# Strassen's seven block products in the second product of an attention and MLP kernel (batches 2 to 7 and the state tokens)

## The chip, the cores and the metric

The kernel runs on one core of a Trainium2 chip. The metric is the device time of one execution in microseconds (us). An engine's name is short for: PE = TensorE, DVE = VectorE, ACT = ScalarE, SP = SyncE, which only issues DMAs here.

## The reference

There are 8 batches of 512 tokens, 8 heads of 64 columns, and 32 state tokens for each batch and head. Tokens attend to the state, and the state attends to the tokens; all 4,608 rows of 512 columns that come out go through an MLP.

```python
scores = x @ state.T / sqrt(D);   a  = softmax(scores);   xread = a @ state
scores2 = state @ x.T / sqrt(D);  a2 = softmax(scores2);  sread = a2 @ x
t = concatenate([xread, sread])            # 8 x (512 + 32) rows of 8 x 64 = 512 columns
h = t @ w_in                               # 512 -> 2048
g = h * tanh(log1p(exp(h)))                # mish
out = g @ w_out                            # 2048 -> 512
```

## The kernel before

**Precision.** Operands of the large products are float32, split into a high part and a low part that TensorE takes (`fp32r`). A product of two such operands is three matmuls: high by high, high by low, low by high. So `gh` and `gl` are the high and low half of the activation `g`, `wo[j][:, :, 1]` and `wo[j][:, :, 0]` those of `w_out`, `swh` and `swl` those of the product named next.

**First product.** `xread @ w_in` is worked out as `a` times (state times `w_in`). `sw_slice` makes the inner product for a slot (32-row matmuls into `swp`, then a cast on ACT to `swh` and a subtraction on DVE to `swl`), and `gemm1` multiplies it by the attention weights, `ah` and `al`, into two banks `ph` of 512 tokens. A slot `j` is 256 of the 2048 hidden columns: two feature chunks of 128. Eight slots make a batch.

**Activation and second product.** ACT takes mish of the two banks into `g` (128x1024, one buffer), DVE casts `g` to `gh` and subtracts to get `gl`, and `gemm2` adds the slot's part of `g @ w_out` to four banks `acc`, one for each tile of 128 tokens: 4 tiles x 2 chunks x 3 matmuls of 512 columns. After slot 7 the banks are copied to `o` and stored. Second products run `LAG` = 2 slots behind the first ones, half of a slot's `acc` in front of a pause, half behind it, and in the pause stand (`beside`) the small groups of the next batch: `swp`, the scores `sc`, the state read `srp`. The state tokens of all batches are gathered (`srds`, turned by `sreads_transposed` into `srT`) and go through `gemm1_s` and four slots of their own between batches 6 and 7.

**Order.** For batch 0 the string `STEPS` is an order by hand of all pieces, DVE and ACT included: `p` a first product, `m` mish and cast of `g`, `lg` its `gl`, `g` a second product, `ji`/`jo`/`lo` joining, casting and splitting a slice of `w_in` or `w_out`, `hi`/`ci`/`di`/`ho`/`co`/`do` roundings of the loaded words. From batch 1 on (`dve.on = act.on = False`) the order on DVE and ACT comes from the scheduler; PE keeps the order of the code. `w_in` joined lies whole in SBUF (`w_in_sb`). All loads and stores go through SP's queue in order.

Of the kernel before, what the change touches and what calls it, by code (L numbers as in the profile page):

```python
# [17 lines left out]
P = 128  # L18
# [67 lines left out]
def state_attention_mish_kernel(ctx, tc, x_turned, x, state_wide, state, w_in, w_out, out):  # L86
# [34 lines left out]
    w_in_sb = const.tile([P, NC, DF], F32, name="w_in_sb")  # L121
# [4 lines left out]
    srT = [const.tile([P, NC, B * NS], F32R, name=f"srT_{n}") for n in ("h", "l")]  # L126
# [56 lines left out]
    def join_w_in(e, raw):  # L183
        join_words(raw, w_in_sb[:, :, e * 2 * P:(e + 1) * 2 * P])
# [142 lines left out]
    def attention(b):  # L327
        aT = {}

        def scores(bank=misc):  # L330
# [8 lines left out]
            soft["sc"] = pool.tile([P, 2, S], F32, tag="sc", name=f"scs_{b}", bufs=2)  # L339
# [54 lines left out]
        def soft1_a():  # L394
# [3 lines left out]
            hi, lo = (pool.tile([P, 2, S], F32R, tag=t, name=f"{t}_{b}") for t in ("ah", "al"))  # L398
# [5 lines left out]
        def softs():  # L404
# [4 lines left out]
            whole(soft1_n(), soft1_a())  # L409
# [17 lines left out]
        def alone(step):  # L427
# [3 lines left out]
            sc=lambda _: scores(second_bank if b == 0 else misc), tr=alone(soft1_t), em=alone(soft2_m), ex=alone(soft1_x),  # L431
            ee=alone(soft2_x), no=alone(soft1_n), pr=alone(soft1_a), tl=alone(soft2_t), sr=sread, aT=aT, softs=softs)
# [3 lines left out]
    def sreads_transposed():  # L436
        for bs in (range(0, 4), range(4, B)):
# [10 lines left out]
    def sw_slice(b, j, n=2, bank=misc):  # L448

        pw = [bank(f"swp_{b}_{j}_{u}")[:, :n * 2 * P] for u in two]  # L450
        for i in range(n):
            f, to = (slice(q * 2 * P, (q + 1) * 2 * P) for q in (j + i, i))
            for c in range(NC):
                o = slice(c * NS, (c + 1) * NS)
                for u in two:
                    last["PE"] = pe.matmul(
                        pw[u][o, to], bd(b, u, c), w_in_sb[half(u), c, f], start=True, stop=True)
        yield
        hi = pool.tile([P, 2, n * 2 * P], F32R, tag="swh", name=f"swh_{b}_{j}", bufs=3)
        lo = pool.tile([P, 2, n * 2 * P], F32R, tag="swl", name=f"swl_{b}_{j}", bufs=3)  # L460
# [314 lines left out]
```

## Time and profile before

| | before |
|---|---|
| median of the runs shown (lowest, highest) | 651.73 us (651.31, 651.95) |
| the profiled execution: its own time / span | 650.5 us / 648.7 us |
| PE busy | 639.4 us, 99% |
| PE weight loads busy (beside matmuls) | 510.1 us, 79% |
| DVE busy | 320.7 us, 49% |
| ACT busy | 234.6 us, 36% |
| granted TensorE clock over the span | 1.000 |

Busy times are those of the profiled execution, over its whole span. A PE that is busy 99% is not thereby at its peak, since matmuls are pipelined and their ends are modelled; how long a stream of them takes is read from where one piece of the chain starts and the next one does. Shares of DVE and ACT are means over stages that differ: they are high in the first 95 us and low later.

### The profile page before, as it was taken

What the parts mean: (1) busy time and instruction counts of PE and PEld (TensorE: products, weight loads), DVE (VectorE), ACT (ScalarE), POOL (GpSimd) and SP (SyncE); (2) the same over time, 40 slices, a digit from 0 to 9 for tenths busy, and PEclk for the clock granted to TensorE, in tenths of its full rate; (3) what the DMA queues carried; (4) which work ended last, traced back from release to release, by engine and by line L of the source; (5) the groups of instructions that cost most, each with busy time, mean ns of one, the idle gap of its engine ahead of it and who ended that gap; (6) DMA issues with size and microseconds to landing.
All of it is one profiled execution on the core that took longest, in us unless ns stands there. A gap on an engine that the chain in (4) does not pass through costs nothing.

```text
span 648.7 us, 10258 instructions
## 1 busy us (share of the span) xinstructions
PE 639.4 (99%) x4380; PEld 510.1 (79%) x4380; DVE 320.7 (49%) x412; ACT 234.6 (36%) x364; POOL 0.7 (0%) x6
## 2 busy tenths in 40 slices
PE   7999999999999999999999999999999999999997
PEld 5776777787778887787778788787778789878886
DVE  5989984293428234543437234742447244332222
ACT  4997862352325122522324213412334234131110
POOL 0000000000000000000000000000000000000000
PEclk9999999999999999999999999999999999999999
DMA  8968115021031003110220003110110001000001
GB/s 329 392 211 337 66 33 204 25 72 28 33 105 68 24 1 130 66 33 1 76 107 27 21 15 116 66 33 1 66 66 23 11 1 66 1 17 17 0 1 65
DMA packets 18573, 47.91 MB, mean 74 GB/s; under 512 B 3424, under 2 KB 7904, under 8 KB 16608
## 3 DMA queue, kind: packets, MB, share of 16 engines
q1 hardware_dynamic: 18384, 47.13, 20.5%
q8 instruction: 34, 0.56, 0.3%
q10 hardware_dynamic: 144, 0.13, 0.1%
q14 instruction: 11, 0.09, 0.0%
HBM read 34.14 MB, written 8.91 MB: 66 GB/s over the span
## 4 chain that ended last, share of the span: by engine, by line
PE 88%; DVE 2%; ACT 2%; issue 1%; DVEq 0%; ACTq 0%
PE acc L78 50%; PE ph L78 24%; PE swp L78 4%; PE acc_s L78 3%; PE ph_s L78 3%; PE srp L78 1%; PE sc L78 1%; ACT L78 1%; DVE w L78 0%; DVE gl L78 0%; ACT g L78 0%; DVE wo L78 0%; ACT wir L78 0%; ACT scs L78 0%; ACT wor L78 0%
## 5 line engine op out<-in xcount | busy, mean ns | idle before, releaser
L78 PE MATMUL acc<-wo,gh 128*128 128x512 f32 (+1 forms) x1028 | 319.5, 392 | 0.0
L78 PEld LDWEIGHTS acc<-wo,gh 128*128 128x128 f32 x1028 | 190.5, 188 | 47.1 <-issue 8.2
L78 PE MATMUL acc<-wo,gl 128*128 128x512 f32 (+1 forms) x514 | 199.9, 389 | 0.1
L78 ACT ACTIVATE g<-ph 128x512 f32<-128x512 f32 x128 | 74.0, 597 | 230.2 <-DVE gl L78 215.9
L78 DVE CAST gh<-g 128x1024 fp32r<-128x1024 f32 x64 | 44.0, 687 | 145.5 <-PE acc L78 141.1
L78 PEld LDWEIGHTS acc<-wo,gl 128*128 128x128 f32 x514 | 96.5, 188 | 21.4 <-DVE gl L78 0.9
L78 DVE TENSOR_TENSOR gl<-g,gh 128x1024 fp32r<-128x1024 f32 x64 | 78.0, 1219 | 4.6
L78 PE MATMUL ph<-ah,swh 128*128 128x512 f32 (+1 forms) x260 | 79.4, 388 | 0.0
L78 PE MATMUL ph<-al,swh 128*128 128x512 f32 (+1 forms) x260 | 78.9, 386 | 0.4 <-DVE al L78 0.4
L78 PE MATMUL ph<-ah,swl 128*128 128x512 f32 (+1 forms) x260 | 78.9, 387 | 0.0
L78 DVE TENSOR_TENSOR swl<-swp,swh 128x512 fp32r<-128x512 f32 (+1 forms) x72 | 41.1, 625 | 64.3 <-ACT swh L78 64.2
L78 PEld LDWEIGHTS ph<-al,swh 128*128 128x128 f32 x260 | 48.4, 188 | 10.5 <-DVE al L78 0.6
L78 PEld LDWEIGHTS ph<-ah,swh 128*128 128x128 f32 x260 | 48.2, 188 | 10.6 <-issue 0.8
L78 PEld LDWEIGHTS ph<-ah,swl 128*128 128x128 f32 x260 | 48.4, 188 | 10.1 <-DVE swl L78 0.2
L78 ACT CAST swh<-swp 128x512 fp32r<-128x512 f32 (+1 forms) x72 | 34.2, 550 | 38.7 <-PE swp L78 38.7
L78 ACT ACT_TABLE_LOAD x27 | 34.6, 1283 | 18.2 <-DVE nm L78 14.7
L78 PE MATMUL swp<-w_in_sb,bds 64*32 64x256 f32 x896 | 28.1, 380 | 0.0
L78 DVE STREAM_TRANSPOSE e<-scs 128x1024 f32<-128x1024 f32 x7 | 8.7, 1244 | 34.6 <-ACT scs L78 34.6
L78 PE MATMUL ph_s<-srT_h,w 128*128 128x256 f32 x128 | 23.9, 286 | 0.4 <-DVE w L78 0.3
L78 ACT COPY o<-acc 128x512 f32<-128x512 f32 (+1 forms) x16 | 9.2, 574 | 40.6 <-PE acc L78 38.7
L78 PEld LDWEIGHTS swp<-w_in_sb,bds 64*32 64x32 f32 x896 | 15.9, 106 | 10.0 <-issue 6.0
L78 DVE COPY o<-acc 128x512 f32<-128x512 f32 (+1 forms) x17 | 11.4, 671 | 21.5 <-PE acc L78 16.1
(64 smaller groups left out, 399.8 us busy)
## 6 DMA issues: line engine op xcount, KB each, us to landing
wir<-in_w_in_dram SPq DMA_DIRECT2D x16, 512.0 KB, 9.1
wor<-in_w_out_dram SPq DMA_DIRECT2D x16, 512.0 KB, 9.3
x<-in_x_dram SPq DMA_DIRECT2D x8, 1024.0 KB, 5.0
out_dram<-o SPq DMA_DIRECT2D x31, 256.0 KB, 2.0
xT<-in_x_turned_dram SPq DMA_DIRECT2D x7, 1024.0 KB, 4.9
e2T<-e2b SPq DMA_DIRECT2D x128, 32.0 KB, 1.9
xT<-in_x_turned_dram SPq DMA_DIRECT2D x2, 512.0 KB, 5.1
out_dram<-o_s SPq DMA_DIRECT2D x2, 256.0 KB, 2.0
```

The costliest lines, as they stand in the source:

```text
L78: made = method(*args, **kwargs)
```

## The change

In batches 2 to 7 and for the state tokens the second product is done in steps (batch, slot, pair `p` of token tiles). In a step the activation is a 2 by 2 block matrix (two tiles of 128 tokens, two chunks of 128 hidden columns) and so is the slice of `w_out` (two chunks, two halves of 256 columns). Strassen's scheme in Winograd's form needs seven products of blocks in place of eight, each again three matmuls, and sums of blocks on both sides:

- `combine_g` forms four sums of 128x128 on DVE, casts the seven left blocks to `gh` on ACT (384 and 512 columns) and subtracts to `gl` on DVE (384 and 512 columns). Mish is now put into unit tiles `gu` by 256 columns.
- `combine_w_out` forms the right blocks once per slot: two adds of 512 columns that bring back `w_out` from its halves, four of 256, four casts on ACT and four subtractions of 256 on DVE.
- `products` are 21 matmuls of 256 columns in place of 12 of 512, and `results` adds the seven sums up at the end of a batch's token pair (five adds of 256 and one of 512 columns on DVE, two copies on ACT).

To make room, `w_in` is no longer kept whole: its eight slices are written to DRAM (`keep_w_in`) and come back two at a time through one buffer (`load_kept`, 1 MB each, four for each of batches 2 to 7 and four for the state tokens). `srT`, `xT` from batch 3 on and `x` share one buffer; `ah`, `al` have one instead of two; `swh`, `swl` two instead of three. First products of a batch stand at steps −2 to 5 of the batch's 16 (slot 0 of batches 3 to 6 at step −8, at the change of token pair of the batch before), `swp` and `sc` at steps of their own. In `STEPS` and `LOADS` pieces change places: three casts of `gh` and two of `wo` go from DVE to ACT (`n`, `ko`), two roundings from ACT to DVE.

```diff
-    w_in_sb = const.tile([P, NC, DF], F32, name="w_in_sb")
+    wi = {}
+    w_in_kept = [dram.tile([P, 2, NC, 2 * P], F32, name=f"w_in_kept_{i}") for i in range(SLOTS // 2)]
...
+    def load_kept():
+        if order:
+            b, i = order.pop(0)
+            w = pool.tile([P, 2, NC, 2 * P], F32, tag="wis", name=f"w_in_{b}_{i}", bufs=1)
+            nc.sync.dma_start(w.rearrange("p j c f -> p (j c f)"), w_in_kept[i].rearrange("p j c f -> p (j c f)"))
+            kept.append(w)
...
+    def combine_w_out(j):
+        w = [new_unit(f"w_{j}_{k}").rearrange("p a n -> p (a n)") for k in two]
+        for k in two:
+            dve.tensor_add(w[k], as_f32(wo[j][:, k, 0]), as_f32(wo[j][:, k, 1]))
+        (b11, b12), (b21, b22) = ((w[k][:, :256], w[k][:, 256:]) for k in two)
...
+        dve.tensor_sub(t1, b12, b11)
+        dve.tensor_sub(t3, b22, b12)
+        dve.tensor_sub(t2, b22, t1)
+        dve.tensor_sub(t4, b21, t2)
+        to = [wo[j][:, 0, :, 256:], wt23[:, 0], wt23[:, 1], wt4[j // 4][:, j % 4]]
+        for part, o in zip((t1, t2, t3, t4), to):
+            act.copy(o[:, 1], part)
+            dve.tensor_sub(o[:, 0], part, as_f32(o[:, 1]))
...
+    def combine_g(step):
+        u = units.pop(step)
...
+        dve.tensor_add(s[:, 0], a21, a22)
+        dve.tensor_sub(s[:, 2], a11, a21)
+        dve.tensor_sub(s[:, 1], s[:, 0], a11)
+        dve.tensor_sub(s[:, 3], a12, s[:, 1])
...
+        for to, of in ((slice(0, 3), u[:, 1:4]), (slice(3, 7), s)):
+            act.copy(gh[:, to], of)
+        for to, of in ((slice(0, 3), u[:, 1:4]), (slice(3, 7), s)):
+            dve.tensor_sub(gl[:, to], of, as_f32(gh[:, to]))
...
+    def products(step, which):
...
+        for name, i in PRODUCTS[which]:
+            bank, side = PLACES[name]
+            o = accs[key, p][bank][:, side * 256:(side + 1) * 256]
+            for n, (g, w) in enumerate(((gh, 1), (gh, 0), (gl, 1))):
+                last["PE"] = pe.matmul(
+                    o, g[:, i], moving[j][name][:, w], start=(j == 0 and n == 0 and side == 0),
+                    stop=(j == SLOTS - 1 and n == 2), skip_group_check=True)
...
+    for b in range(2, B):
+        plan = dict(sw4=-1 if b > 2 else 0, sc=0, sw6=2)
+        if b < B - 1:
+            plan.update(last=5, sw0=6, sw2=10 if b < B - 2 else 8, sr=10 if b < B - 2 else 8)
...
+    for k in range(-LAG, len(steps)):
+        for f in firsts.get(k, ()):
+            first_of(*f)
...
+        if k + 1 < len(steps):
+            combine_g(steps[k + 1])
...
+        products(steps[k], slice(0, 4))
+        together(*beside)
+        products(steps[k], slice(4, 7))
+        with behind("swl"):
+            for f in after:
+                f()
+        for f in loads:
+            f()
+        key, j, p = steps[k]
+        if j == SLOTS - 1:
+            results(key, p)
```

What the change moves on DVE at the end of batch 0 is not in the diff, since the scheduler places `combine_w_out`. Before, these rows of DVE lead up to `gl_7`, the low half of batch 0's last slot (`w_7` joins the last slice of `w_out`, `rs`, `sm`, `e2b` belong to softmax, `swl_1_0` to the first `swp` of batch 1):

```order
L78 STREAM_TRANSPOSE e2b_0_897<-scs_0_217 128x8x4x32
L78 TENSOR_TENSOR al_1_782<-at_1_778,ah_1_781 128x1024
L78 SCALAR_TENSOR_TENSOR w_7_849<-wor_7_141 128x1024
L78 RECIPROCAL rs_0_893<-sm_0_769 128x2
L78 CAST wo_7_851<-w_7_849 128x2x512
L78 TENSOR_TENSOR swl_1_0_825<-swp_1_0_0_806,swh_1_0_824 128x512
L78 TENSOR_TENSOR swl_1_0_825<-swp_1_0_1_807,swh_1_0_824 128x512
L78 CAST gh_0_7_855<-g_0_7_834 128x1024
L78 TENSOR_TENSOR wo_7_851<-w_7_849,wo_7_851 128x2x512
L78 TENSOR_SCALAR sm_1_860<-sm_1_860 128x2
L78 STREAM_TRANSPOSE e2b_1_1086<-scs_1_683 128x8x4x32
L78 TENSOR_TENSOR gl_0_7_856<-g_0_7_834,gh_0_7_855 128x1024
```

Now the rows that end in the same `gl_7` are these (`gu_t_4` are sums of blocks of `w_out` for slot 4, `wt23` low halves of the right blocks of slots 0 and 1):

```order
L79 RECIPROCAL rs_0_910<-sm_0_767 128x2
L79 TENSOR_TENSOR wt23_0_1104<-gu_t_0_1_1102,wt23_0_1104 128x256
L79 TENSOR_TENSOR wt23_0_1104<-gu_t_0_0_1101,wt23_0_1104 128x256
L79 CAST wo_7_854<-w_7_852 128x2x512
L79 TENSOR_TENSOR swl_1_0_833<-swp_1_0_0_814,swh_1_0_832 128x512
L79 TENSOR_TENSOR swl_1_0_833<-swp_1_0_1_815,swh_1_0_832 128x512
L79 TENSOR_TENSOR wt23_1_1240<-gu_t_1_1_1239,wt23_1_1240 128x256
L79 TENSOR_TENSOR wt23_1_1240<-gu_t_1_0_1238,wt23_1_1240 128x256
L79 TENSOR_TENSOR gu_t_4_0_1521<-gu_w_4_0_1517 128x256
L79 TENSOR_TENSOR gu_t_4_0_1521<-gu_w_4_1_1518,gu_w_4_0_1517 128x256
L79 TENSOR_TENSOR wo_7_854<-w_7_852,wo_7_854 128x2x512
L79 TENSOR_TENSOR gl_0_7_866<-g_0_7_836,gh_0_7_865 128x1024
```

Six operations of `combine_w_out` stand in the second piece, the cast of `g_7` has gone to ACT and one `sm` with its `e2b` behind `gl_7`; further up, 30 more of them stand between the pieces of batch 0.

On ACT, at the scores of batch 4 in the middle of batch 3, the rows before are these (`g_3_j` mish of slot j, `scs` scores and their exponentials, `e1` those of the tokens):

```order
L78 ACTIVATE g_3_3_2306<-ph_3_3_0_2292 128x512
L78 ACTIVATE g_3_3_2306<-ph_3_3_1_2293 128x512
L78 ACTIVATE scs_4_2368<-sc_4_0_2325 128x512
L78 ACTIVATE scs_4_2368<-sc_4_1_2326 128x512
L78 ACT_TABLE_LOAD
L78 ACTIVATE scs_4_2368,sm_4_2395<-scs_4_2368,nm_4_2392 128x512 x2
L78 ACTIVATE e1_4_2385<-e1_4_2385 128x1024
L78 ACT_TABLE_LOAD
L78 ACTIVATE g_3_4_2444<-ph_3_4_0_2430 128x512
```

Now they are (`gu_3_j_p` mish of slot j for token pair p, `gh_3_2_0` the casts of a step):

```order
L79 ACTIVATE scs_4_2833<-sc_4_0_2823 128x512
L79 ACTIVATE scs_4_2833<-sc_4_1_2824 128x512
L79 CAST gh_3_2_0_2911<-gu_3_2_0_2790 128x384
L79 CAST gh_3_2_0_2911<-s_3_2_0_2906 128x512
L79 ACTIVATE gu_3_3_0_2900<-ph_3_3_0_2886 128x256
L79 ACTIVATE gu_3_3_1_2903<-ph_3_3_0_2886 128x256
L79 ACT_TABLE_LOAD
L79 ACTIVATE scs_4_2833,sm_4_2855<-scs_4_2833,nm_4_2852 128x512 x2
L79 ACT_TABLE_LOAD
L79 ACTIVATE gu_3_3_0_2900<-ph_3_3_1_2887 128x256
L79 ACTIVATE gu_3_3_1_2903<-ph_3_3_1_2887 128x256
```

Mish of a slot's second bank, `ph_3_3_1`, has come to stand behind the exponentials and a second table load; before, mish of both banks of slot 3 stood ahead of the scores.

SP's queue at the end of batch 1, before:

```order
L131 DMA x_1_1080<-in_x_dram 128x2048
L369 DMA e2T_1_1083<-e2b_1_1086 32x256 x16
L131 DMA x_2_1382<-in_x_dram 128x2048
L369 DMA e2T_2_1316<-e2b_2_1319 32x256 x16
L583 DMA out_0_dram<-o_1_0_1594 128x512
L583 DMA out_0_dram<-o_1_1_1603 128x512
L583 DMA out_0_dram<-o_1_2_1660 128x512
L583 DMA out_0_dram<-o_1_3_1669 128x512
```

and now:

```order
L134 DMA x_2_1406<-in_x_dram 128x2048
L373 DMA e2T_2_1383<-e2b_2_1386 32x256 x16
L464 DMA w_in_2_1_1660<-w_in_kept_1_79 128x2048
L147 DMA xT_3_1662<-in_x_turned_dram 128x2048
L696 DMA out_0_dram<-o_1_0_1759 128x512
L696 DMA out_0_dram<-o_1_1_1768 128x512
L696 DMA out_0_dram<-o_1_2_1777 128x512
L696 DMA out_0_dram<-o_1_3_1786 128x512
L464 DMA w_in_2_2_1832<-w_in_kept_2_80 128x2048
L464 DMA w_in_2_3_1977<-w_in_kept_3_81 128x2048
L134 DMA x_3_1979<-in_x_dram 128x2048
L373 DMA e2T_3_1956<-e2b_3_1959 32x256 x16
```

Three loads of `w_in` slices stand where there was none, two of them behind the stores of batch 1.

## Rows read from the trace of the kernel before

**Rows 1.** The page: busy time and share of each engine (part 1), and the shares of the chain that ended last by engine (part 4).

```profile
PE 639.4 (99%) x4380; PEld 510.1 (79%) x4380; DVE 320.7 (49%) x412; ACT 234.6 (36%) x364; POOL 0.7 (0%) x6
...
PE 88%; DVE 2%; ACT 2%; issue 1%; DVEq 0%; ACTq 0%
```

**Rows 2.** The chain that ended last in order of time, batches 2 to 4: start us, us, what, number of instructions.

```profile
163.34 1.02 PE swp L78 x32
...
299.88 2.99 PE acc L78 x12
302.87 2.72 PE ph L78 x12
305.59 5.44 PE acc L78 x24
...
316.47 1.89 PE swp L78 x64
...
334.94 1.02 PE sc L78 x16
...
371.79 2.99 PE acc L78 x12
```

**Rows 3.** Stretches: from:to, length, then busy time and number of instructions of PE, PE's weight loads, DVE, ACT and POOL, granted TensorE clock, DMA share, GB/s.

```profile
40.00:60.00 20.00, 19.68 (x124) 14.29 (x123) 17.88 (x23) 17.63 (x24) 0.00 (x0) 1.00 0.99 348
60.00:80.00 20.00, 19.86 (x111) 14.68 (x110) 19.69 (x25) 14.61 (x20) 0.00 (x0) 1.00 0.29 108
300.00:350.00 50.00, 50.00 (x345) 39.80 (x345) 25.44 (x35) 17.24 (x29) 0.00 (x0) 1.00 0.18 64
```

**Rows 4.** The timeline near 25 us and up to the end of batch 0 (DVE, and the weight load of PE that waits for `gl_7`): start us, us, engine, line, operation, out<-in, count; in brackets the idle time before and what ended it. Where a count is 2, the us are of both.

```profile
24.64 0.75 DVE L78 TENSOR_TENSOR swl<-swp,swh 128x256 fp32r<-128x256 f32 x2
25.30 1.21 DVE L78 TENSOR_TENSOR gl<-g,gh 128x1024 fp32r<-128x1024 f32 x1
26.92 1.22 DVE L78 SCALAR_TENSOR_TENSOR w_in_sb<-wir 128x1024 uint32<-128x1024 uint32 x1 [0.40 <-ACT wir L78]
...
86.81 1.28 DVE L78 TENSOR_TENSOR swl<-swp,swh 128x512 fp32r<-128x512 f32 x2
88.01 0.68 DVE L78 CAST gh<-g 128x1024 fp32r<-128x1024 f32 x1
88.61 1.22 DVE L78 TENSOR_TENSOR wo<-w,wo 128x1024 fp32r<-128x1024 f32 x1
90.29 0.17 DVE L78 TENSOR_SCALAR sm<-sm 128x2 f32<-128x2 f32 x1 [0.46 <-ACT scs L78]
90.36 1.24 DVE L78 STREAM_TRANSPOSE e2b<-scs 128x1024 f32<-128x1024 f32 x1
91.53 1.18 DVE L78 TENSOR_TENSOR gl<-g,gh 128x1024 fp32r<-128x1024 f32 x1
...
92.76 0.19 PEld L78 LDWEIGHTS acc<-wo,gl 128*128 128x128 f32 x1 [0.50 <-DVE gl L78]
```

**Rows 5.** The chain in order of time, a first product of the state tokens.

```profile
554.23 5.77 PE ph_s L78 x48
```

**Rows 6.** Groups of DVE instructions by shape: line, engine, operation, out<-in, shapes, count, busy us, mean ns of one, idle us before them and what ended it.

```profile
L78 DVE TENSOR_TENSOR gl<-g,gh 128x1024 fp32r<-128x1024 f32 x64 | 78.0, 1219 | 4.6
L78 DVE CAST gh<-g 128x1024 fp32r<-128x1024 f32 x64 | 44.0, 687 | 145.5 <-PE acc L78 141.1 <-ACT g L78 3.1 <-PE acc_s L78 1.2
L78 DVE TENSOR_TENSOR swl<-swp,swh 128x512 fp32r<-128x512 f32 x56 | 35.1, 684 | 62.0 <-ACT swh L78 62.0
...
L78 DVE TENSOR_TENSOR swl<-swp,swh 128x256 fp32r<-128x256 f32 x16 | 6.0, 417 | 2.3 <-ACT swh L78 2.2
```

**Rows 7.** The timeline from the scores of batch 4 to the end of its exponentials: as rows 4.

```profile
264.03 1.10 PE L78 MATMUL srp<-x,e2T 128*32 128x64 f32 x64
264.19 1.09 ACT L78 ACTIVATE scs<-sc 128x512 f32<-128x512 f32 x2 [3.19 <-PE sc L78]
...
265.31 1.25 DVE L78 STREAM_TRANSPOSE e<-scs 128x1024 f32<-128x1024 f32 x1 [5.76 <-ACT scs L78]
...
266.48 1.18 DVE L78 TENSOR_REDUCE nm<-scs 128x2 f32<-128x1024 f32 x1
...
267.73 1.28 ACT L78 ACT_TABLE_LOAD   x1 [2.45 <-DVE nm L78]
...
270.36 0.19 ACT L78 ACTIVATION_READ_ACCUMULATOR scs<-scs,nm 128x1 f32 x1
```

**Rows 8.** Groups of ACT instructions by shape: as rows 6.

```profile
L78 ACT ACT_TABLE_LOAD x27 | 34.6, 1283 | 18.2 <-DVE nm L78 14.7 <-DVE rs L78 2.6
...
L78 ACT CAST swh<-swp 128x256 fp32r<-128x256 f32 x16 | 5.1, 377 | 2.6 <-PE swp L78 2.6
```

**Rows 9.** DMA issues of the page: out<-in, queue, count, KB each, median us from issue to landing.

```profile
out_dram<-o SPq DMA_DIRECT2D x31, 256.0 KB, 2.0
xT<-in_x_turned_dram SPq DMA_DIRECT2D x7, 1024.0 KB, 4.9
```

**Rows 10.** The timeline near the end, weight loads beside 256-column matmuls: as rows 4.

```profile
643.62 0.19 PEld L78 LDWEIGHTS acc<-wo,gl 128*128 128x128 f32 x1
643.74 0.28 PE L78 MATMUL acc<-wo,gl 128*128 128x256 f32 x1
643.74 0.31 PEld L78 LDWEIGHTS acc<-wo,gh 128*128 128x128 f32 x2
```

More of the change, by code (lines that the diff above doesn't have):

```diff
@@ L408, in softs @@
             soft2_x()
-            whole(soft1_n(), soft1_a())
+            whole(soft1_n())
             soft2_t()
@@ L684, in state_attention_mish_kernel @@
+    for j in range(SLOTS):
         g = split_g(f"{key}_{j}", mish(key, j, gemm1(key, j, aTs[key], sw)))
         pending.append((key, (2 * j, 2 * j + 1), g, NT))
-        slow = key == 1 and j < 2
-        ready = slow or len(pending) > LAG
-        n = pending[0][3] // 2
-        if ready and not slow:
-            second(range(n), True)
-        more = key + 1 < B
-        if j == 0 and more:
-            atts[key + 1] = attention(key + 1)
-            aTs[key + 1] = atts[key + 1]["aT"]
-        own, following = atts[key], atts.get(key + 1)
@@ L697, in state_attention_mish_kernel @@
-        if key == 1 and j == 0:
+        slow = j < 2
+        done = pending[0]
+        if not slow:
+            second((0, 1), True)
+        if j == 0:
+            atts[2] = attention(2)
+            aTs[2] = atts[2]["aT"]
             atts[0]["tl"](0)
         beside = []
-        if key == 1 and j == 1:
+        if j == 1:
             beside += [sw_slice(key, 2)]
-        if j == (3 if key == 1 else 1):
+        if j == 2:
+            beside += [atts[0]["sr"](u) for u in two]
+        if j == 3:
@@ L715, in state_attention_mish_kernel @@
-        if j == (4 if key == 1 else 3) and key < B - 1:
-            beside += [own["sr"](u) for u in two]
-        if key == B - 2 and j == 7:
-            beside += [following["sr"](u) for u in two]
+        if j == 4:
+            beside += [atts[2]["sc"](0)] + [atts[1]["sr"](u) for u in two]
+        if j == 7:
+            beside += [sw_slice(2, 0, kept=kept.pop(0))] + [atts[2]["sr"](u) for u in two]
         together(*beside)
-        if ready:
-            second((2 * j, 2 * j + 1), j == 0) if slow else second(range(n, 2 * n))
@@ L722, in state_attention_mish_kernel @@
-        if key == 1 and j == 2:
+        second((2 * j, 2 * j + 1), j == 0) if slow else second((2, 3))
+        if done[0] == 1:
+            combine_w_out(done[1][0] // 2)
+        if j == 2:
             xss[1] = load_x(1)
-            own["tl"](0)
-        if more and j == (4 if key == 1 else 3):
+            atts[1]["tl"](0)
+        if j == 4:
             with behind("swl"):
-                following["softs"]()
-        if key + 2 < B and j == 2:
-            with behind("store"):
-                xTs[key + 2] = load_xT(key + 2)
@@ L731, in state_attention_mish_kernel @@
-        if key < B - 1 and j == (5 if key == 1 else 4):
-            with behind("mish"):
-                xss[key + 1] = load_x(key + 1)
-    while pending:
-        second()
+                atts[2]["softs"]()
+            load_kept()
+            xss[2] = load_x(2)
+        if j == 7:
+            load_kept()
+            xTs[3] = load_xT(3)
+            atts[2]["last"]()
+    steps, base = [], {}
+    for b in (*range(2, B - 1), "s", B - 1):
+        base[b] = len(steps)
+        steps += [(b, j, p) for p in range(1 if b == "s" else 2) for j in range(SLOTS)]
```

201 lines of the change are left out of this document (137 added, 64 removed).

## Prediction

> **What bounds the kernel now.** I read the page first, then the chain of waits, then stretches, then single rows. TensorE (PE) is busy 99% of the 648.7 us span and holds 88% of the chain that ended last [rows 1]. The chain shows why. From batch 2 on a batch repeats every 371.79 − 299.88 = 71.91 us, and its pieces follow each other without a hole [rows 2]: eight slots, each of a first product (`ph`, 12 matmuls of 512 columns, 2.72 us) and a second one (`acc`, 24 matmuls, 5.44 us), 8.16 us together, and groups of 32-row matmuls (`swp`, `sc`, `srp`) that make up the rest. A 512-column matmul therefore costs 2.72 / 12 = 226.7 ns, and what the other engines do in these batches is hidden as long as it is ready in time.
>
> The other stage is batch 0, where weights are still being joined, split and rounded. There VectorE (DVE) is busy 17.88 of 20 us (40 to 60 us) and 19.69 of 20 us (60 to 80 us), against 25.44 of 50 us in a later batch [rows 3]. PE waits for it until late: the last low half of batch 0, `gl_7`, runs from 91.53 for 1.18 us on DVE, and the weight load that reads it starts at 92.76, after 0.50 us idle, named as DVE's [rows 4]. So a microsecond of PE counts anywhere after 92.76 us, and a microsecond of DVE counts before it.
>
> **The change, part by part.**
>
> *Fewer matmul columns.* A step (batch, slot, token pair) had 12 matmuls of 512 columns and gets 21 of 256. The nearest row for the new kind is `ph_s`, 48 matmuls of 256 columns, each with a weight load of its own, in 5.77 us: 120.2 ns [rows 5]. A step takes 21 × 0.1202 = 2.524 instead of 2.72 us, 0.196 less. Six batches have 16 steps and the state tokens 8: 104 × 0.196 = **−20.4 us**. Bounds: half of the 512-column time, 113.3 ns, would give 2.38 and −35 us; the small fixed part in 120.2 against 113.3 is what two dense stretches show, so I take 120.2.
>
> The Trainium skill, page "TensorE: Matmul & The Clock Gate", section "Back-to-back issue gap", speaks against halves: it gives about 81 ns for 128 and 131 ns for 512 columns in a stream of weight loads and matmuls; on the line between them 256 columns are, as an estimate, 98 ns, so that 21 of them (2.06 us) would cost more than 12 wide ones (1.57). This trace does not agree: it has 226.7 and 120.2 ns, a ratio of 0.53 and not 0.75.
>
> *More groups of 32-row matmuls.* A `swp` of two slices costs 1.02 us alone and 1.89 with its neighbour, and the `acc` that follows a group takes 2.99 instead of the half of 5.44 [rows 2]. The change places `swp_0`, `swp_2`, `swp_4`, `swp_6` and `sc` at steps of their own: 4 × 1.02 − 2 × 1.89 = 0.30 and two more groups at 0.27, 0.84 a batch. Four batches at 0.84 and batches 2 and 7, whose `swp` were partly apart already, with one group more each: 3.4 + 0.5 = **+3.9 us** (0, if narrow neighbours pay no such entry, to 4).
>
> *The combinations of w_out.* They stand in no loop that waits for them, and the scheduler has put five of eight partly into batch 0. The order of DVE up to `gl_7` gains ten adds of 512 columns and 26 of 256, loses three 1024-column casts on balance (five casts to ACT, two roundings from it), and one transposition with a small operation moves behind `gl_7`. From start to start a pair of 512 took 88.01 − 86.81 = 1.20, so 0.60 each; a pair of 256 took 0.66, so 0.33 each; a cast 0.60; the transposition 1.17 [rows 4]. The sum is 6.0 + 8.6 − 1.8 − 1.3 = 11.5 us. What of it is hidden? DVE's idle time between 26 and 91 us is six waits, from 0.40 at 26.92 to 0.46 at 90.29, 3.7 us together; gaps between its instructions may take another 2.5. So `gl_7` comes 11.5 − 3.7 = 7.8 us later, 5.3 if the gaps close too, 11.5 if the waits for ACT remain. PE's order around it is unchanged, so PE stands for as long. I take **+7.5 us**. The rest of the combinations falls into batch 1, where DVE has half its time free.
>
> *Work per step on DVE.* Casts and `gl` of a slot were 0.687 + 1.219 us [rows 6] for 5.44 us of PE. Now each step has four adds of 128 columns and subtractions of 384 and 512. By the line through 0.417 us at 256 and 0.684 at 512 columns, 128 cost 0.284 and 384 0.55, an estimate: 4 × 0.284 + 0.55 + 0.684 = 2.37 us for 2.524 of PE, or for 5.24 where a first product stands beside the step. This is the new thin place. It costs nothing in steady steps, since `gh` and `gl` have two buffers and run one step ahead; whatever delays DVE or ACT by more than about 0.7 us now shows on PE.
>
> *New waits that follow.* I went along the queues from place to place:
> - A. Softmax, batches 2 to 6. ScalarE (ACT) holds mish of `ph_3` second half behind the softmax of the next batch, and `ph_4` needs that bank. From the end of `sc` (264.03 in the old batch) the chain scores, transposition, maximum, table, exponentials ends at 270.55, 6.5 us later; a table load of 1.28 and two mish of 256 columns follow, 0.38 by the row of another 256-column operation: 8.6 [rows 7, 8]. PE gets there after 9 + 21 products, `ph_3` and half of `ph_4`: 1.33 + 2.52 + 2.72 + 1.36 = 7.93. Some 0.65 is missing each time, 3.2 us in five batches; before, a slot's 5.44 us lay between instead of 2.52.
> - B. `w_in` is reloaded through one buffer. In batch 2 the load for `swp_4` starts when `swp_2` has been read. A load of 1 MB lands in 4.9 us [rows 9], and PE has `ph_2_2` and four products, 4.4 us: 0.5 us if the queue issues at once, 2.5 if a store of 2.0 us [rows 9] is in front; 2.0.
> - C. Batch 6: `srTp` needs `srds`, which DVE has behind a whole step's work (2.37, some 1.9 after its cover), and one `gl` is ordered ahead of the one needed first, 1.2: 3.1.
> - D. State tokens: three reloads of 4.9 with cast and subtraction behind (0.6 + 0.68) against two steps and the last matmuls of `ph_s` (5.05 + 0.6): 3 × 0.55 = 1.7.
> - E. Batch 7 has no first products in its second half: 1.4 at the change of token pair, where the additions of the results meet the next bank, and 4 × 0.37 in the last steps, where DVE subtracts before it forms the sums that ACT waits for: 2.9.
>
> Together 12.9 us. Each is worked out as though PE came there undelayed, so one covers part of the next, and the lower end of each is 0 (B apart). I take the middle, **+6.5 us** (0.5 to 13).
>
> **The sum.** 650.5 is the profiled execution's own time (span 648.7). 650.5 − 20.4 + 3.9 + 7.5 + 6.5 = 648.0; the median of the runs, 651.73, lies 1.2 above the profiled one: **649 us**, 0.4% less.
>
> **The rivals.**
> 1. *The waits come in full or more* (sum of A to E 13, batch 0 up to 11.5): 650.5 − 20.4 + 3.9 + 8 + 13 = 655, with 11.5 658.5; on the median's scale 656 to 660. For it: these waits share one cause, ACT and DVE serving two lines of work without reserve. Against: PE's delays give them time back. It decides from 9.0 us of waits on (the time of before) and is slower by what can be told from 10.3, that is, when four of the five come whole.
> 2. *The waits are hidden*: 650.5 − 20.4 + 3.9 + 5.3 + 1 = 640.3, with the median's 1.2 641.5. For it: DVE has half its time free in old batches [rows 3]. Faster.
> 3. *DVE becomes the bound of a step.* If a 128-column add costs what the row of 256 says, 0.417, a step is 4 × 0.417 + 1.23 = 2.90 on DVE against 2.524 on PE. In the eight steps of a batch without a first product 0.38 is missing each: 3 us a batch, some 20 us with state tokens, about 668. Against it: the two rows lie on a line with little fixed part.
> 4. *The weight load is not hidden behind 256 columns.* A load is 0.19 us long; were it not overlapped, a step would take 21 × 0.19 = 3.99, 1.27 more, 132 us in all, and 780 us. Against it: loads of 0.19 and their matmuls start every 0.12 us [rows 10]. This is the mechanism of the page cited above; by its ratio of 0.75 a step would be 3.57 us and the time some 88 us longer than before.
> 5. *Narrow matmuls at half the wide ones' time*: −35 instead of −20.4, 634. No row shows it; the fixed part would have to vanish.
>
> **How the numbers follow.** About 0.2% (1.3 us, 650.4 to 653.0) is what this kernel's runs can tell from no change. The forecast, 645 to 653, has 0.41 (of it 0.26 faster, 0.12 same, 0.03 slower); rival 1 0.25; rival 2 0.23; rival 3 0.06; rival 4 0.02; rival 5 0.03. Faster 0.26 + 0.23 + 0.03 = 0.52, same 0.12, slower 0.36. The range, 639.5 to 659, takes in the forecast and most of rivals 1 and 2.
>
> **What would show it.** `acc` pieces of 21 matmuls at 2.5 us in the chain (if 2.4 or 2.7, the first term). `gl_7` on DVE at about 99 us, with PE's wait before it (third term). A wait of PE in `ph_4` for ACT's mish, 0.6 us, in each of batches 2 to 6; one in `swp_4` of batch 2 for a DMA. DVE at 85 to 90% in the middle batches: if it is 95% and PE waits in steps 6 to 13 for `gl`, rival 3 holds. The prediction is wrong if the wait at `gl_7` is under 4 us, or if waits after it add up to under 2 or over 12.

## The result, and the profile after

The changed kernel takes 657.46 us (median; 657.23 to 659.87) against 651.52 of the kernel before on the same chip: ratio 1.0099, 95% interval 1.0075 to 1.0124. It is 0.9% slower. 649 us, 0.4% faster, had been forecast; the time lies inside the range, on the other side. The profiled execution took 657.69 us, its span is 655.9 (before 648.7). Of the runs further down, one of the four of e10 fell into a slower state (687.3 us at a granted clock of 0.851) and is left out there.

The page of the changed kernel, its parts 1, 2 (granted TensorE clock in 40 slices) and 4, beside [rows 1]:

```profile
PE 629.1 (96%) x5306; PEld 538.7 (82%) x5306; DVE 494.1 (75%) x1073; ACT 375.8 (57%) x726; POOL 0.7 (0%) x6
...
PEclk9989999999999999999999999999999999999999
...
PE 73%; DVE 10%; DMA 7%; ACT 7%; issue 2%; SPq 0%; DVEq 0%; ACTq 0%
```

PE is busy 10 us less and the span is 7 us longer; DVE has gone from 49 to 75%. The chain that ended last lies on PE for 73% of the span instead of 88%, and DMAs, which had no share worth printing, now hold 7%.

The chain in order of time, batches 3 and 4 of the changed kernel (start us, us, what, count), beside [rows 2]:

```profile
290.51 3.95 PE acc L79 x33
...
302.03 6.47 PE acc L79 x54
...
321.90 2.75 PE ph L79 x12
...
331.12 1.43 PE acc L79 x12
332.55 1.13 PE sc L79 x16
335.95 1.19 DVE nm L79
337.20 1.28 ACT L79
338.50 1.52 ACT scs L79 x4
340.04 1.28 ACT L79
342.04 1.66 PE ph L79 x6
...
360.69 3.95 PE acc L79 x33
```

A batch repeats every 360.69 − 290.51 = 70.18 us, 1.73 less than before. `acc` runs at 6.47 / 54 = 0.120 us a matmul, as taken. After `sc` the chain leaves PE: maximum, table load, exponentials, second table load, and only then the second half of `ph` (6 matmuls at 342.04).

Where the time went is seen from when each batch's third first product (`ph_2`, which stands ahead of the batch's first second product in both kernels) starts in the timeline:

| start, us | before | after | difference | change since the row above (stage) |
|---|---|---|---|---|
| batch 1 | 101.85 | 109.57 | +7.72 | +7.72 (batch 0) |
| batch 2 | 177.46 | 186.19 | +8.73 | +1.01 (batch 1) |
| batch 3 | 249.32 | 258.01 | +8.69 | −0.04 (batch 2) |
| batch 4 | 321.18 | 328.21 | +7.03 | −1.66 (batch 3) |
| batch 5 | 393.09 | 398.39 | +5.30 | −1.73 (batch 4) |
| batch 6 | 464.97 | 468.59 | +3.62 | −1.68 (batch 5) |
| batch 7 | 585.03 | 588.45 | +3.42 | −0.20 (batch 6 and state tokens) |
| last matmul (start + 0.12) | 644.94 | 649.45 | +4.51 | +1.09 (batch 7) |
| end of the span | 648.72 | 655.91 | +7.19 | +2.68 (the end) |

Sixteen steps at 2.51 instead of 2.72 us should give 3.4 us in each batch. Half of that comes through in batches 3 to 5, next to nothing in batches 2, 6 and the state tokens, and batch 7 loses.

The stretches of [rows 3], after (columns as there):

```profile
40.00:60.00 20.00, 20.00 (x120) 14.75 (x107) 19.56 (x30) 17.41 (x21) 0.00 (x0) 0.91 0.96 341
60.00:80.00 20.00, 17.78 (x102) 13.18 (x101) 19.66 (x26) 12.23 (x17) 0.00 (x0) 1.00 0.72 260
300.00:350.00 50.00, 49.44 (x476) 43.19 (x476) 38.48 (x93) 31.04 (x63) 0.00 (x0) 1.00 0.32 114
```

In batch 0 DVE is full, as forecast, and PE idles 2.2 us of 60 to 80. What had not been forecast is a granted clock of 0.91 between 40 and 60 us, the mean of a short stretch at 0.50, shown at the end, and of the rest at 1.00. In a later batch DVE is busy 38.48 of 50 us, not 25.44.

The end of batch 0 in the timeline, beside [rows 4]:

```profile
99.21 1.22 DVE L79 TENSOR_TENSOR gl<-g,gh 128x1024 fp32r<-128x1024 f32 x1
...
100.48 0.19 PEld L79 LDWEIGHTS acc<-wo,gl 128*128 128x128 f32 x1 [0.95 <-DVE gl L79]
```

`gl_7` starts at 99.21 instead of 91.53, and PE's weight load behind it at 100.48 instead of 92.76. It waits only 0.95 us for it; PE came late already, as `sc` of batch 1 shows in the timeline, before and after:

```profile
64.04 1.42 PE L78 MATMUL sc<-xT,bds 64*32 64x512 f32 x16
...
68.94 1.09 PE L79 MATMUL sc<-xT,bds 64*32 64x512 f32 x16 [2.22 <-DVE swl L79]
```

PE's waits (engine, group, what it waited for: us in total, times, longest):

```profile
PE swp L79 <- DVE w_in L79: 3.1, 2, 1.8
PE ph L79 <- ACT gu L79: 2.9, 5, 0.7
PE sc L79 <- DVE swl L79: 2.2, 1, 2.2
PE sc L79 <- DMA xT<-in_x_turned_dram: 2.1, 1, 2.1
PE acc L79 <- DVE gl L79: 2.0, 6, 0.6
...
PE acc L79 <- DVE o L79: 1.3, 3, 0.9
PE ph L79 <- ACT swh L79: 1.3, 2, 0.9
...
PE ph_s L79 <- DVE w L79: 0.8, 1, 0.8
PE srTp L79 <- DVE srds L79: 0.7, 1, 0.7
```

The first line is of batch 0. The wait of 2.2 us for `swl` is that of `sc` at 68.94; the wait for `xT` is that of the very first `sc`, at 5.96 us, and the kernel before has it too (2.20 us).

Groups of DVE's instructions by shape on the page, beside [rows 6]:

```profile
L79 DVE TENSOR_TENSOR gl<-s,gh 128x512 fp32r<-128x512 f32 x96 | 66.3, 691 | 20.4 <-ACT gh L79 20.2
...
L79 DVE TENSOR_TENSOR gl<-gu,gh 128x384 fp32r<-128x384 f32 x96 | 53.0, 552 | 26.0 <-ACT gh L79 25.3
L79 DVE TENSOR_TENSOR s<-gu 128x128 f32<-128x128 f32 x192 | 49.1, 289 | 21.0 <-ACT gu L79 16.6
```

128 columns cost 0.289 us and 384 0.552; 0.284 and 0.55 had been estimated.

The end, PE, DVE and SP in the timeline:

```profile
649.33 0.28 PE L79 MATMUL acc<-wt,gl 128*128 128x256 f32 x1
649.95 0.42 DVE L79 TENSOR_TENSOR o<-o,o 128x256 f32<-128x256 f32 x1
...
650.76 1.01 DVE L79 TENSOR_TENSOR o<-o,acc 128x512 f32<-128x512 f32 x2
...
652.20 0.41 SPq L655 DMA_DIRECT2D out_dram<-o  x1
```

The last matmul starts at 649.33, the additions of the results end at 651.77, the last store of 256 KB is issued at 652.20. Before, 3.8 us passed from the last matmul to the end of the span; now 6.5 do.

### The profile page after: what moved, and what is told of

Read it like the earlier page. It is cut to its first block, busy times and chain, and to the rows that moved or that the text cites. A ratio compares the mean times of both kernels' runs of the same rounds, so it can differ in the third digit from the quotient of the medians.

```text
span 655.9 us, 13371 instructions
## 1 busy us (share of the span) xinstructions
PE 629.1 (96%) x5306; PEld 538.7 (82%) x5306; DVE 494.1 (75%) x1073; ACT 375.8 (57%) x726; POOL 0.7 (0%) x6
## 4 chain that ended last, share of the span: by engine, by line
PE 73%; DVE 10%; DMA 7%; ACT 7%; issue 2%; SPq 0%; DVEq 0%; ACTq 0%
PE acc L79 40%; PE ph L79 21%; PE swp L79 4%; PE acc_s L79 3%; PE ph_s L79 2%; ACT L79 2%; DVE gl L79 2%; DMA w_in_s<-w_in_kept 2%; ACT scs L79 2%; DMA wor<-in_w_out_dram 2%; DMA wir<-in_w_in_dram 1%; PE srp L79 1%; PE sc L79 1%; DVE w L79 1%; DVE o L79 1%
## 5 line engine op out<-in xcount | busy, mean ns | idle before, releaser
L79 PE MATMUL acc<-wo,gh 128*128 128x256 f32 (+1 forms) x1024 | 231.3, 314 | 0.9 <-DVE o L79 0.9
L79 PE MATMUL acc<-wo,gl 128*128 128x256 f32 (+1 forms) x512 | 159.2, 311 | 1.3 <-DVE gl L79 1.3
L79 PE MATMUL acc<-wt,gh 128*128 128x256 f32 x576 | 112.6, 284 | 0.9 <-ACT gh L79 0.5
L79 PEld LDWEIGHTS acc<-wt,gh 128*128 128x128 f32 x576 | 89.7, 192 | 1.6 <-DVE o L79 0.8
L79 ACT ACTIVATE gu<-ph 128x256 f32<-128x256 f32 x192 | 63.5, 384 | 35.8 <-PE ph L79 34.7
L79 PE MATMUL acc<-wt,gl 128*128 128x256 f32 x288 | 82.1, 285 | 0.8 <-DVE gl L79 0.7
L79 DVE TENSOR_TENSOR gl<-s,gh 128x512 fp32r<-128x512 f32 x96 | 66.3, 691 | 20.4 <-ACT gh L79 20.2
L79 ACT CAST gh<-s 128x512 fp32r<-128x512 f32 x96 | 59.3, 618 | 37.0 <-DVE s L79 36.9
L79 DVE TENSOR_TENSOR gl<-gu,gh 128x384 fp32r<-128x384 f32 x96 | 53.0, 552 | 26.0 <-ACT gh L79 25.3
L79 PEld LDWEIGHTS acc<-wt,gl 128*128 128x128 f32 x288 | 55.2, 192 | 2.0 <-DVE gl L79 2.0
```

Of the source, the lines that this page charges most:

```text
L79: made = method(*args, **kwargs)
```

## The experiments

The theory after this reading: every wait of the list A to E costs its whole price, so that half of them was the wrong sum. Rivals: the waits share slack and a repaired one only uncovers the next; or DVE's amount of work sets the pace; or batch 0 is held by something else than DVE's sums. Two of the runs leave out part of the computation, as they say.

Beside the experiments the kernel before took 650.57 to 650.93 us, not 651.52, so two totals that differ by less than 1 us can't be told apart. What an edit did is therefore read stage by stage too, between the starts of `ph_2` in the profiled execution. Two stages vary there without an edit to them: batch 0 (see e3), and batch 6 with the state tokens, by up to 0.7 us.

**e1: combinations behind `gl_7`.**

```diff
+    gl_7 = dve.last
...
-            combine_w_out(done[1][0] // 2)
+            with tc.issue_after(gl_7):
+                combine_w_out(done[1][0] // 2)
...
```

> The combinations of w_out are queued on DVE behind gl_7 of batch 0; nothing else is changed. Theory (each microsecond of DVE before gl_7 is one of PE): gl_7 ends near 93 us in place of 100.4, and the time falls by 7.3 us to about 650.2, less what the 11.5 us of work cost in batch 1, where DVE is busy about 70% of the time. Rival (batch 0 is held by something else in this kernel, its loads or ACT, so that the combinations only filled holes): gl_7 ends at 98 us or later and the time stays within 2 us of 657.5. Second rival (the work is needed so soon that the loss moves): gl_7 ends near 93, PE waits 4 us or more in batch 1 or at the start of batch 2, and the time is 654 or more.

658.19 us (657.85 to 660.26): no gain at all, the second rival, with a part of the first. `gl_7` started at 94.34, not 91.5, because another wait had come to light. The timeline of e1, SP, PE and DVE:

```profile
54.14 0.33 SPq L147 DMA_DIRECT2D xT<-in_x_turned_dram  x1
...
66.71 1.51 PE L79 MATMUL sc<-xT,bds 64*32 64x512 f32 x16 [4.27 <-issue]
...
70.68 0.69 DVE L79 CAST gh<-g 128x1024 fp32r<-128x1024 f32 x1 [6.77 <-PE acc L79]
```

Two loads of `x_turned` were issued here, and took 12.5 and 6.4 us to land. The first is that of batch 1, issued at 54.14: it landed at 66.6 us, and `sc` starts at 66.71. The view names nothing that ended PE's 4.27 us, but the landing fits, and e7 bears it out; DVE stood 6.77 us behind PE. In the changed kernel itself the same load is just as late. This is its group for the tile `xT` between 45 and 75 us (first and last start; then SP's issues, then time to landing):

```profile
L79 PE MATMUL sc<-xT,bds x16: 586/589/614, 68.9 to 69.4; 64*32 64x512 f32 x16
L147 SPq DMA_DIRECT2D xT<-in_x_turned_dram x2: 328/328/328, 58.4 to 70.1; - x2
...
DMA to landing us min/median/max: 5.9/8.2/10.5
```

The first of the two loads is again the slow one: 58.37 + 10.5 = 68.9, and `sc` starts at 68.94, put down to DVE's `swl`, which ends at 68.82. So batch 0 seems to have two bounds of one height, DVE's sums and the load; e5 to e7 put that to the test. What e1 won by then (`gl_7` at 94.34, 4.9 us ahead of the changed kernel's) it lost in batch 1, where the combinations stood in one block ahead of that batch's first `gl`: still 2.8 us ahead at `ph_2` of batch 1, it is 0.84 us behind at `ph_2` of batch 2.

**e5: loads only.** xT_1 ahead of x_0, stores of the `w_in` slices behind all loads.

```diff
-    i0 i1 o0 o1 i2 i3 o2 i4 i5 o3 o5 i6 o4 x0 i7 s1 o6 t1 o7
+    i0 i1 o0 o1 i2 i3 o2 i4 i5 o3 o5 i6 o4 i7 s1 o6 t1 o7 x0
...
-    for e in range(SLOTS):
-        keep_w_in(e)
+    with behind("load"):
+        for e in range(SLOTS):
+            keep_w_in(e)
```

> In the loads of batch 0 xT_1 stands ahead of x_0, and the eight stores of w_in slices stand behind all loads; the combinations stay where the change had them. Theory (batch 0 has two bounds of nearly one height, DVE with the combinations and the arrival of xT_1, so that taking one away uncovers the other): the wait of sc for xT_1 goes, DVE still reaches gl_7 at 99 to 101 us, and the time stays within 2 us of 657.5. Rival (the arrival of xT_1 alone held batch 0): gl_7 ends by 96 and the time falls by 4 or more.

657.39 us (656.11 to 658.40), `gl_7` at 98.72: the theory. The load now landed 6.6 us after its issue at 57.95, `sc` still started at 68.12, behind DVE alone. Which of the edit's two halves sped the load up, its place or that of the stores, no run separates.

**e6: combinations spread over batch 1.**

```diff
-            combine_w_out(done[1][0] // 2)
+            with tc.issue_after(dve.last):
+                combine_w_out(done[1][0] // 2)
...
```

> The combinations of slot j are queued on DVE behind what the program has traced when slot j of batch 1 is done, one slot's at a time over batch 1; the loads stay as the change has them. Theory: batch 0 as in the run where they all stood behind gl_7, held by xT_1 (sc at 66 to 67 us, gl_7 at 94 to 96), but batch 1 without the 5.8 us that it lost there, since they no longer stand in one block ahead of its gl_0; the time falls by 4 to 5 to about 653. Rival (batch 1 has no room for 11.5 us wherever they stand, DVE being busy some 70% of it): PE still loses 4 us or more in batch 1 and the time stays above 656.

656.46 us (654.79 to 656.99): 1.0 gained at most, not 4 to 5. Batch 0 went as expected (`sc` at 67.23, `gl_7` at 94.73), and batch 1 kept 2.5 us of the gain up to `swp_2` at its end. There PE waited 1.8 us for `swh` by the wait list, not 0.9, and a stretch of lower granted clock followed (0.51 from 186.2 to 189.6 us; in e8, below, it is seen alone). At the `acc` behind it e6 was 0.5 us later than the changed kernel: the whole gain was given back at the start of batch 2. The expectation missed that.

**e7: loads and spreading together.**

> Both edits together: xT_1 ahead of x_0, the stores behind the loads, the combinations spread over batch 1. Theory (two bounds): both are gone, gl_7 ends at 92 to 94 us as before the change, and the time falls by 7 us to about 650.5, more than the two alone together. Rival: one bound only, the gain is that of the better of the two alone.

650.27 us (648.93 to 650.81), 7.2 less, where the two alone gave 0.1 and 1.0: two bounds, and the theory's number. At `ph_2` of batch 1 it is plainer: e5 is there 0.5 us ahead of the changed kernel, e6 2.4 us, and e7 9.3 us. (The profiled execution is one of the two shortest of ten, 648.95 us.) Its timeline, SP and PE:

```profile
53.08 0.33 SPq L147 DMA_DIRECT2D xT<-in_x_turned_dram  x1
...
61.80 1.09 PE L79 MATMUL sc<-xT,bds 64*32 64x512 f32 x16
```

`gl_7` and the weight load that reads it, in the timeline:

```profile
87.87 1.22 DVE L79 TENSOR_TENSOR gl<-g,gh 128x1024 fp32r<-128x1024 f32 x1
...
91.11 0.19 PEld L79 LDWEIGHTS acc<-wo,gl 128*128 128x128 f32 x1
```

The load landed 7.4 us after its issue, at 60.4, and PE does not wait for `sc` at all. `gl_7` ends at 89.1, some 3 us earlier than the 92 to 94 that had been expected, and PE reads it 2 us later without a wait: neither bound holds PE there any more. At `ph_2` of batch 1 this kernel is at 100.29, ahead of the kernel before (101.85).

**e2: softmax behind mish** (wait A).

```diff
+    late = []
...
+        with behind("mish"):
+            while late:
+                late.pop(0)()
...
-        with behind("swl"):
-            for f in after:
-                f()
+        late += after
```

> The softmax of the next batch is queued on ACT behind mish of both banks of slot 3, in batches 2 to 6; nothing else is changed. Theory (waits of this kind add up whole): the five waits of ph for mish, 0.72 to 0.82 us over a matmul's pace each, 3.7 us together, are gone and the time falls by about 3.7 to 653.8. Rival (they cover waits that follow them, which is why I took half): they are gone too, other waits of PE in the same batches grow, and the time falls by less than 2.

654.82 us (653.95 to 658.14), 2.6 less, which lies between the theory and the rival (by the ratios to the kernel before, 1.0070 and 1.0099, it is 1.9). The stages say more. The wait of `ph` for mish, 2.9 us in five pieces by the wait list, is gone: `ph_4` takes 2.75 us, in the changed kernel 3.70 in batch 2 and 3.62 in batches 3 to 6. But the two first products behind it take 2.97 and 2.79 us instead of 2.75, where a shorter wait for mish stands now (0.35 us at 277.04). So batches 2 to 5 are shorter by 0.45, 0.61, 0.59 and 0.61 us: a half to 70% of the wait came back, and the rest was uncovered one slot later. That the last matmul of the profiled execution, the shortest of the four, comes 3.67 us earlier is luck: 1.2 of it are from batch 6 with the state tokens and 0.2 from batch 0.

**e3: sums ahead of `gl`** (part of C and E).

```diff
-        dve.tensor_sub(s[:, 3], a12, s[:, 1])
+        formed = dve.tensor_sub(s[:, 3], a12, s[:, 1])
...
-        for to, of in ((slice(0, 3), u[:, 1:4]), (slice(3, 7), s)):
-            dve.tensor_sub(gl[:, to], of, as_f32(gh[:, to]))
+        with tc.issue_after(getattr(formed, "ins", formed)):
+            for to, of in ((slice(0, 3), u[:, 1:4]), (slice(3, 7), s)):
+                dve.tensor_sub(gl[:, to], of, as_f32(gh[:, to]))
```

> On DVE each step's four sums are queued ahead of its two subtractions for gl; nothing else is changed. Theory: the waits of PE for gl and gh in batch 6 from 521 us and in the last half of batch 7 (eight of 0.2 to 0.7 us, 3.2 together) come from that order and go; the time falls by 2 to 3.5. Rival (DVE's amount of work sets them, 2.4 of 2.5 us in a step): they stay within a third and the time changes by less than 1.

656.56 us (655.87 to 659.44), 0.9 less. By stages: batch 0 was 1.3 us later in the profiled execution, batch 6 with the state tokens 1.8 us shorter, batch 7 1.3 us shorter. The 3.1 of the last two are what was expected; the total alone would not have told it. Batch 0 was later too in e4 and e10 (2.3 and 1.2 us), with the order of the changed kernel there. The granted clock accounts for most of it: right behind `sc` it is 0.50 in these three (68.5 to 71.9 us in e3, 69.8 to 73.2 in e4, 68.4 to 71.8 in e10) and 1.00 in the changed kernel, e2 and e5, and from the start of `sc` to that of `gl_7` the three take 31.7 to 31.8 us, the others 30.3 to 30.6. PE had waited 2.4 to 3.2 us for `sc` in the three; in the changed kernel and in e2 it was 2.2. In e4 `sc` itself also started 0.75 us later, as its load landed at 69.6.

**e4: reloads left out.** The kernel leaves the second loads of the slices out and uses one slice pair in place of them all.

```diff
+            if kept_one:
+                kept.append(kept_one[0])
+                return
...
+            kept_one.append(w)
```

> Leaves out the reloads of w_in: one slice pair is loaded once and used for all (the products get the wrong slices). Theory: the waits near the reloads (0.37 us in batch 2, some 2 in the first products of the state tokens) go, and the time falls by 2 to 3. Rival (the reloads slow more than the chain shows, by traffic beside loads of x and the stores): it falls by 5 or more. Second rival (those waits belong to the casts of the slices on ACT and DVE): less than 1.

656.46 us (653.28 to 656.67). Batch 0 was 2.3 us later, batch 6 with the state tokens 2.9 us shorter, batches 2 to 5 as they were. So the reloads cost about 3 us (0.7 more or less), nearly all of it in the state tokens, and their traffic slows nothing in batches 2 to 5; the total alone, 1.0 less, would not have told that.

**e10: sums left out.** One addition of 512 columns stands for the four sums.

```diff
-        dve.tensor_add(s[:, 0], a21, a22)
-        dve.tensor_sub(s[:, 2], a11, a21)
-        dve.tensor_sub(s[:, 1], s[:, 0], a11)
-        dve.tensor_sub(s[:, 3], a12, s[:, 1])
+        dve.tensor_add(s, u, u)
```

> The kernel of the change, but the four sums of a step are left out: one addition of 512 columns stands in their place, which is not Strassen's sum. DVE has 0.5 to 0.6 us less work in each of 104 steps. Theory (the waits come from order and from chains between engines, and DVE is no bound of a step): the time falls by 1 to 3 us, in the waits of the last batch and of batch 6. Rival (DVE's 2.4 us of work in a step of 2.5 set the pace): it falls by 8 or more.

656.93 us (655.45 to 658.13), no measurable change. Its page:

```profile
PE 628.8 (96%) x5306; PEld 539.4 (82%) x5306; DVE 464.4 (71%) x761; ACT 373.6 (57%) x726; POOL 0.7 (0%) x6
```

DVE has 30 us less work, 0.29 us a step and not the 0.5 to 0.6 expected, and batches 2 to 5 take as long as in the changed kernel or up to 0.4 us longer. Rival 3 of the prediction, DVE as the bound of a step, is out; even the 1 to 3 us that I had expected did not come.

**e8: all repairs**, e7, e2 and e3 together, and in the very last step p5 ahead of p6 and p7.

> The last run's edits, the softmax behind mish, the sums ahead of gl, and in the very last step the product p5 ahead of p6 and p7, so that the additions at the end start 0.7 us earlier. Theory (waits add up whole): 650.5 less 3.6, less 1, less 0.7, about 645, faster than the kernel before the change by some 6 us. Rival (each repaired wait uncovers the next one): 648 or more.

644.05 us (643.70 to 645.40), ratio 0.9902 (0.9887 to 0.9917) to the kernel before: faster than it, by what the theory says. The medians of e7 and e8 are 6.2 us apart; the stages of the profiled executions show 3.6 of them, since e7's (648.95) is short and e8's (645.40) is the longest of its four, so the sum isn't shown term by term. Of the end, 0.3 us came, not 0.7, and kernels without this edit differ there by as much. One wait stood out in the timeline of its PE, in front of `ph_2` of batch 2:

```profile
174.95 1.09 PE L79 MATMUL swp<-w_in,bds 64*32 64x256 f32 x32
177.83 1.28 PE L79 MATMUL ph<-ah,swh 128*128 128x512 f32 x2 [1.78 <-ACT swh L79]
178.91 1.05 PE L79 MATMUL ph<-al,swh 128*128 128x512 f32 x2
```

Stretches of e8 around it (columns of [rows 3], the granted clock behind POOL's):

```profile
174.00:178.00 4.00, 2.22 (x38) 1.18 (x36) 4.00 (x9) 2.94 (x7) 0.00 (x0) 1.00 0.54 187
178.20:181.40 3.20, 3.20 (x8) 2.28 (x8) 2.56 (x7) 1.29 (x5) 0.00 (x0) 0.50 0.81 302
181.60:185.00 3.40, 3.40 (x57) 2.84 (x63) 0.88 (x3) 0.66 (x2) 0.00 (x0) 1.00 0.00 0
```

PE waits 1.78 us for `swh` and had 2.22 of 4 us busy; then the granted clock is 0.50 (1.2 of 2.4 GHz) and a pair of 512-column matmuls takes some 0.9 us from start to start, not 0.45.

**e9: `swp_2` amid the second product**, in addition to e8.

```diff
-                second()
+                second((0, 1), True)
+                if k == -1:
+                    whole(sw_slice(2, 2, kept=kept.pop(0)))
+                    load_kept()
+                second((2, 3))
...
-                whole(sw_slice(2, 2, kept=kept.pop(0)))
-                load_kept()
```

> The kernel with all repairs, and the swp_2 of batch 2 stands in the middle of the second product ahead of it and not right in front of ph_2. Theory: PE's wait of 2.0 us in front of ph_2 goes, and with it the 3.4 us at half the granted clock that follow it (seven pairs of matmuls at 0.43 in place of 0.23 us each, some 1.6 us); the time falls by 3 to 4 to about 640.5. Rival (the granted clock falls for a reason of its own): only the wait goes, the half-clock stretch stays in or moves, and the time falls by 2 or less.

640.09 us (639.91 to 640.48), ratio 0.9835 (0.9820 to 0.9850) to the kernel before. The same place:

```profile
174.00:178.00 4.00, 4.00 (x20) 3.29 (x19) 3.90 (x8) 2.07 (x5) 0.00 (x0) 1.00 0.99 327
178.00:182.00 4.00, 4.00 (x65) 2.94 (x63) 3.75 (x12) 2.93 (x9) 0.00 (x0) 1.00 0.31 120
```

No idle PE, no half clock. The gain is 4.0 us for a wait of 1.8: the theory. In the profiled executions `ph_2` of batch 2 comes 1.7 us earlier and batch 2 is 1.9 shorter, 3.6 together; another 1.9 lie in batch 6 with the state tokens, which the edit doesn't touch, and aren't explained. This is the fastest version of this study, with the same matmuls, casts and sums as the change; only their order differs.

## Why the prediction was wrong, by its own steps

| term, us | forecast | measured | read from |
|---|---|---|---|
| products | −20.4 | −21.6 | 104 steps, 2.72 to 2.51 us |
| groups of 32-row matmuls | +3.9 | +2.4 | the groups and what the `acc` beside them lose; +0.5 a batch in 3 to 5, not 0.84 |
| batch 0 | +7.5 | +7.7 | `gl_7`'s weight load, 92.76 to 100.48 |
| waits A to E, whole | 12.9 | 14.1 | pieces of PE's stream over the same pieces without a wait |
| the share of them that counts | 6.5 | all | the changed kernel's own trace |
| the end | 0 | +2.7 | last matmul to end of span |
| first products | 0 | +1.3 | 48 × 12 matmuls, 0.2289 for 0.2267 us |

The measured column is read from starts in the timelines, from `ph_2` of batch 1 on.

**The step that failed** is "Each is worked out as though PE came there undelayed, so one covers part of the next ... I take the middle". In the changed kernel's trace no wait was shortened by another: by the pieces that hold them (a first product takes 2.75 us, a step 2.51, a group 1.02 where PE doesn't wait) A cost 0.95 + 4 × 0.87 = 4.4 (3.2 forecast), B 1.5 (2.0), C 3.3 (3.1), D 1.9 (1.7), E 3.0 (2.9), and batch 1 lost another 0.9. The forecast of each was near; halving their sum was the error. The reason is argued, and read from the chain for A alone: they are chains through ACT, DVE or a DMA that begin with a piece of PE's own work (`sc`, `swp`, a free bank), so when PE comes later, the chain begins later too, and has the same length against the same cover. With the whole 12.9 the prediction's own sum is 655.6 on the median's scale. That a wait costs its whole length does not mean that its repair gives it all back: e2 got back 0.6 of 0.87 us a batch.

**What was left out.** The end: additions of the results that follow one another on DVE, and a last store of 256 KB where the kernel before had cut its last one in two; 2.7 us in no term, and no run tests that cause by itself. Batch 1's 0.9, 0.4 at the change of token pair in batch 6 and the first products' 1.3, whose cause is open, are not in the sum either. The measured terms, −21.6 + 2.4 + 7.7 + 14.1 + 0.9 + 0.4 + 2.7 + 1.3, add up to 7.9; less 0.9 that the kernel before had waited in the state tokens that is 7.0 of the 7.2 us by which the span grew.

**Right, for half the reason.** Batch 0's +7.5 came out at +7.7, and `gl_7` at 99 us as named. But "PE's order around it is unchanged, so PE stands for as long" took DVE as the only bound. The load of xT_1, moved behind x_0 and mixed with the stores of `w_in`, had come up to the same height; e1 and e5, each of which takes one bound away, gain nothing in the total, and e7 gains 7.2. The prediction had called itself wrong if PE's wait at `gl_7` was under 4 us, and it is 0.95: of the 7.7 us 4.9 were lost ahead of `sc` already. So the number is in part luck. B was placed right but named wrong: of 1.5 us the reload is 0.3, the rest is PE's wait for ACT's `swh`, since `swp_2` stands right in front of `ph_2` (e9).

**Right.** The price of a narrow matmul: 0.120 us, still 0.53 of a wide one's 0.2267, so rival 4 is out, as is rival 5. The Trainium skill, page "TensorE: Matmul & The Clock Gate", section "Back-to-back issue gap", gives about 131 ns a matmul at 512 columns in a stream of weight loads and matmuls; these traces, with 227 ns, don't agree. Rival 1, "the waits come in full or more", is what happened: 656 to 660 had been given for it, with a chance of 0.25. Its deciding point, 9.0 us of waits, was passed, and so was the 12 that the prediction had named as its own refutation. DVE in the middle batches, forecast at 85 to 90%, is at 77% (38.48 of 50 us); it was its place in the chains that counted, not its fullness.

## What to carry to other kernels

When waits are traced one by one and each begins with the bound engine's own work, add them up whole: lateness of that engine moves their beginning too, and does not pay for them. Expect less from a repair, since it can uncover the next wait of its kind. Where a stage is full on one engine, look at what lands at the same moment, since undoing one of two equal bounds shows nothing, and each alone will then look innocent. A cut in the bound engine's work is won or lost in the order around it: the same matmuls took 657.5 us and, with seven edits of order, 640.1.

## What the runs showed of the hardware that had not been expected

The granted TensorE clock fell to 0.50 behind some waits of PE: in e8 as shown above, in e9, without that wait, not at that place, and in the changed kernel between 40.2 and 43.5 us, after 2.12 of 4 us busy (stretches of the changed kernel, columns of [rows 3]):

```profile
36.00:40.00 4.00, 2.12 (x16) 1.15 (x22) 4.00 (x7) 2.37 (x3) 0.00 (x0) 1.00 0.03 12
40.20:43.50 3.30, 3.30 (x23) 2.25 (x8) 3.30 (x6) 2.72 (x4) 0.00 (x0) 0.50 0.78 259
```

It did not fall behind each of them. In e7's profiled execution PE waited 1.77 us at e8's place and was busy 2.23 of 4 us (173.9 to 177.9), and the granted clock stayed at 1.00. Why it fell in one and not in the other no run shows. Taking away the wait of 1.8 us that e8 had gained 4.0 us. The kernel before had no such stretch ahead of its last matmul, so none of this could be read from its trace.

A load of 1 MB that lands in 4.9 us by the median of the kernel before [rows 9] took 10.5 us in the changed kernel and 12.5 in e1, while loads and stores of weights were under way (DMA shares of 0.96 to 1.03 in the stretches around). The share alone does not tell: in e7, with the load one place ahead and the stores behind, it took 7.4 us at shares of 0.78 to 0.99.
